# Loading the values of fourteen of sixteen heads through a second DMA queue in a decode attention kernel

## Chip, cores, metric

One core of one Trainium2 chip; the other cores do nothing. The metric is the device time of one execution in microseconds (us). A kernel's time is the median over its runs. The span of a profile, from the first to the last instruction of one profiled execution, is some 1.8 us shorter than the measured time of the same execution.

## The reference, cut to what matters

```python
# x: 2 x 1 x 448; caches: 2 batches x 8 kv heads x 32768 x 256; 16 query heads; bf16
W = 4096                                    # only the last 4096 positions are attended
xn = layernorm(x)
q = (xn @ wq)                               # 448 x 4096
k, v = k_cache[:, :, Sk - W:], v_cache[:, :, Sk - W:]
p = softmax(q @ k.T * Dh ** -0.5)           # each kv head serves two query heads
A = (p @ v) @ wo                            # 4096 x 448
h = xn @ w1 + b1                            # dense part, 448 x 1792
B = (h * tanh(softplus(h))) @ w2
out = x + A + B
```

There are 8 kv heads x 2 batches = 16 "heads" in the kernel, each with one key tile and one value tile of 4096 x 256 bf16, 2.1 MB each. With wq, w1, w2 and wo (0.46 MB for every second head) 77.9 MB have to be read.

## The kernel before

SP (the synchronisation engine, `nc.sync`, which here does nothing but issue transfers) issues all large loads in one order. Keys have 4 buffers and are loaded two heads ahead; values have 5. The timelines show each engine at its own instructions in the order of the program.

```python
k_pool = tc.tile_pool(name="kk", bufs=4)
v_pool = tc.tile_pool(name="vv", bufs=5)     # wq, w1, w2 use these buffers first
...
def load_v(i, cuts=(0, T)):
    ...
    for lo, hi in zip(cuts, cuts[1:]):
        nc.sync.dma_start(out=t[:, lo:hi, :], in_=vin[:, lo:hi, :])
...
for i in range(NK + KA):                     # NK = 16 heads, KA = 2
    if i + 2 < NK:
        load_k(i + 2)                        # nc.sync
    if i < NK:
        load_v(i, ...)                       # the last head's values in three pieces
        if b == Bsz - 1:
            load_wo(kvh, ...)                # nc.sync, every second head
        for half in range(NH):               # two halves of a head
            s = i * NH + half
            turn(s + 1)                      # VectorE: transpose of the NEXT half's keys (L364)
            scores(s)                        # TensorE: 8 matmuls (L376), ACT: exp (L386)
            turn_p(s - 1)                    # VectorE: transpose of p (L397)
            ...
    ...
    if i >= KA:                              # values of head i-2: TensorE, L431
        ...                                  # (last four heads: 64 small matmuls, L479)
    ...                                      # ACT copies o (L439); later wo (L214)
```

The values of head i are used two iterations after its scores.

The softmax here doesn't subtract the row's maximum and nothing guards it: scores larger than these inputs give would overflow.

## Time and profile before

| | before |
|---|---|
| time, median | 190.46 us (190.43 to 190.48) |
| span | 188.7 us |
| bytes | 77.86 MB, 413 GB/s over the span |
| busy: TensorE, VectorE, ACT | 76%, 60%, 17% |
| keys of heads 13, 14, 15 land | 147.80, 158.67, 168.39 us |
| last value piece lands | 184.27 us |

Two rows of the page show how long a transfer stands in line. The columns are: tiles, issuing queue and operation, count, KB each, median us from issue to landing.

```profile
k<-in_A_k_cache_dram SPq DMA_DIRECT2D x16, 2048.0 KB, 31.5
v<-in_A_v_cache_dram SPq DMA_DIRECT2D x15, 2048.0 KB, 34.8
```

A 2.1 MB tile takes 4.9 us at 430 GB/s; over 30 us to landing means that five to six tiles stand before it. The DMA engines are the bound, and one queue keeps them full. The other views (forty slices, the chain of waits, the timelines of VectorE and TensorE) are in the prediction below.

Names in what follows: k14 and v14 are the key and value tile of head 14, counted from 0. "k14 lands" is the start of the first transpose of that tile, where the profile says that VectorE waited for it.

### The profile page before, as it was taken

Reading aid. Unit: us, or ns where it says so; the run is one execution under the profiler, and the core shown is the slowest. Engines: PE = TensorE matmul, PEld = TensorE weight load, DVE = VectorE, ACT = ScalarE, POOL = GpSimd, SP = SyncE. Lnnn points to the kernel's source line nnn. Section 1 sums busy time; section 2 is a strip of 40 time slices with the busy share of each in tenths; the row PEclk is TensorE's granted clock in tenths of the full one; section 3 lists DMA queues with packets and bytes.
Section 4 is the critical chain, followed back from the end, with each engine's and each line's share of the span. In section 5 each row is a group of like instructions: output and inputs, shape, how many; then the busy total and the mean of one; then the engine's idle time right before and its main releaser. Section 6 shows DMA issues by size and latency. Waiting matters only on the chain.

```text
span 188.7 us, 2944 instructions
## 1 busy us (share of the span) xinstructions
PE 144.1 (76%) x1158; PEld 71.7 (38%) x1158; DVE 113.5 (60%) x195; ACT 32.5 (17%) x82; POOL 27.1 (14%) x139
## 2 busy tenths in 40 slices
PE   0152991788995799869985999769986999597782
PEld 0042390234442345334432434324533443254671
DVE  7805505997919392857649381939376673939401
ACT  2300110112212022111222112202311121211101
POOL 8004430033030022003030203003110300000000
PEclk9999995799999699988999699969998799969955
DMA  6999999999999999999999999999999999999991
GB/s 216 423 432 422 430 430 434 438 431 420 417 441 431 420 416 438 441 427 405 442 434 429 434 420 431 434 431 420 431 431 438 412 432 434 431 441 417 408 394 49
DMA packets 7816, 77.86 MB, mean 413 GB/s; under 512 B 757, under 2 KB 2809, under 8 KB 3322
## 3 DMA queue, kind: packets, MB, share of 16 engines
q1 hardware_dynamic: 7796, 77.66, 97.3%
q8 instruction: 9, 0.15, 0.3%
q14 instruction: 5, 0.04, 0.1%
q10 hardware_dynamic: 6, 0.01, 0.0%
HBM read 77.67 MB, written 0.00 MB: 412 GB/s over the span
## 4 chain that ended last, share of the span: by engine, by line
DMA 82%; DVE 11%; issue 2%; PE 2%; SPq 1%; ACT 0%; ACTq 0%
DMA k<-in_A_k_cache_dram 68%; DMA v<-in_A_v_cache_dram 14%; DVE kt L364 8%; DVE pT L397 2%; PE sc L376 1%; SPq L114 0%; PE psA L214 0%; SPq L338 0%; PE q L479 0%; SPq L280 0%; DVE sums L407 0%; SPq L275 0%; DVE sums L404 0%; DVE den_sb L320 0%; ACT p L386 0%
## 5 line engine op out<-in xcount | busy, mean ns | idle before, releaser
L364 DVE STREAM_TRANSPOSE kt<-k 128x2048 f32<-128x2048 f32 x32 | 73.4, 2296 | 50.6 <-DMA k<-in_A_k_cache_dram 49.6
L376 PE MATMUL sc<-kt,qdiag 128*128 128x512 bf16 x256 | 72.7, 433 | 17.6 <-DVE kt L364 15.8
L376 PEld LDWEIGHTS <-qdiag 128*128 128x128 bf16 x256 | 24.7, 105 | 57.2 <-issue 30.0
L431 PE MATMUL o<-v,pT 128*4 128x512 bf16 x192 | 43.4, 379 | 0.0
L264 POOL COPY qdiag<-qrep 32x8 bf16<-32x8 bf16 x128 | 23.1, 213 | 122.4 <-PE sc L376 107.6
L386 ACT ACTIVATE p<-sc 128x512 bf16<-128x512 f32 x32 | 19.1, 597 | 95.6 <-PE sc L376 93.1
L431 PEld LDWEIGHTS <-pT 128*4 128x4 bf16 x192 | 15.8, 87 | 21.8
L397 DVE STREAM_TRANSPOSE pT<-p 128x512 bf16<-128x512 bf16 x32 | 21.5, 672 | 1.1 <-ACT p L386 1.1
L439 ACT COPY o_sb<-o 4x512 f32<-4x512 f32 x12 | 6.9, 574 | 36.8 <-PE o L431 36.8
L214 PE MATMUL psA<-wo,oT 128*2 128x112 bf16 x128 | 3.8, 245 | 11.0 <-DVE oT L447 11.0
L479 PE MATMUL q<-pT,v 128*128 128x2 bf16 x256 | 7.6, 165 | 1.7 <-DMA v<-in_A_v_cache_dram 1.6
L460 PEld LDWEIGHTS q<-ident_f,o_sb 4*128 4x128 f32 x48 | 6.6, 206 | 5.1 <-issue 5.1
L479 PEld LDWEIGHTS <-v 128*128 128x128 bf16 x256 | 7.3, 101 | 2.0 <-DMA v<-in_A_v_cache_dram 2.0
L414 PEld LDWEIGHTS den<-sums,ones_f 128*128 128x128 f32 x32 | 6.8, 220 | 3.3 <-issue 1.7
L460 PE MATMUL q<-ident_f,o_sb 4*128 4x4 f32 x48 | 7.6, 261 | 0.0
L235 PE MATMUL qT_ps<-xs,v 128*128 128x4 bf16 x112 | 3.3, 166 | 4.8 <-DVE ones L201 2.8
L214 PEld LDWEIGHTS <-oT 128*2 128x2 bf16 x128 | 1.8, 87 | 11.9 <-DVE oT L447 11.7
L386 ACT ACTIVATION_READ_ACCUMULATOR p<-sc 128x1 f32 x32 | 6.2, 194 | 0.0
L177 PE MATMUL xnT_ps<-ident,xn_bf 2*128 2x2 bf16 x7 | 0.5, 167 | 6.3 <-DVE xn_bf L139 6.3
L414 PE MATMUL den<-sums,ones_f 128*128 128x2 f32 x32 | 5.1, 229 | 0.0
L235 PEld LDWEIGHTS <-v 128*128 128x128 bf16 x112 | 3.1, 104 | 5.0 <-issue 3.0
L462 DVE COPY osum<-q 128x4 f32<-128x4 f32 x12 | 1.9, 158 | 3.9 <-PE q L460 3.9
(52 smaller groups left out, 46.5 us busy)
## 6 DMA issues: line engine op xcount, KB each, us to landing
k<-in_A_k_cache_dram SPq DMA_DIRECT2D x16, 2048.0 KB, 31.5
v<-in_A_v_cache_dram SPq DMA_DIRECT2D x15, 2048.0 KB, 34.8
v<-in_B_w_dram SPq DMA_DIRECT2D x2, 1568.0 KB, 21.0
wo<-in_A_wo_dram SPq DMA_DIRECT2D x7, 448.0 KB, 31.5
v<-in_A_wq_dram SPq DMA_DIRECT2D x1, 2048.0 KB
v<-in_A_wq_dram SPq DMA_DIRECT2D x1, 1536.0 KB, 10.8
v<-in_A_v_cache_dram SPq DMA_DIRECT2D x1, 1024.0 KB, 29.1
v<-in_A_v_cache_dram SPq DMA_DIRECT2D x2, 512.0 KB, 27.4
```

Of the source, the lines that this page charges most:

```text
L214: nc.tensor.matmul(part(n), lhsT=lhsT, rhs=w[:, n * DO : (n + 1) * DO], start=start, stop=stop, tile_position=(0, n * Q), skip_group_check ...
L235: nc.tensor.matmul(qT_ps[:, hh, e, :], lhsT=wq_v[s][:, hh, e, :], rhs=xs[:, s, :, :].rearrange("p x b -> p (x b)"), start=(s == 0), stop=( ...
L264: nc.gpsimd.tensor_copy(out=tv[rows, :, e, j * Q : (j + 1) * Q : HS], in_=qrep[rows, :, h0 : h0 + rep, e, x, b],)
L364: nc.vector.transpose(out=kt[:].bitcast(FP32), in_=k[:, half * TH * Dh : (half + 1) * TH * Dh].bitcast(FP32),)
L376: nc.tensor.matmul(psc[:], lhsT=qdiag[i % NW][:, n * NE + e, :], rhs=ktv[:, n, e, :, :], start=(n == 0 and e == 0), stop=(n == NB - 1 and ...
L386: nc.scalar.activation(out=p_sb[:], in_=psc[:].rearrange("p t c -> p (t c)"), func=ACT.Exp, scale=scale, accum_out=state["rs", i][:, s % N ...
L397: nc.vector.transpose(out=pT[:], in_=p_t.pop(s)[:])
L414: nc.tensor.matmul(den[:], lhsT=ones_f[:], rhs=state.pop(("sums", i))[:], start=True, stop=True)
L431: nc.tensor.matmul(po[:], lhsT=pT_t[i * NH + half][:, uh * NP * Q : (uh + 1) * NP * Q : HS], rhs=v[:, u * NP : (u + 1) * NP, :].rearrange( ...
L439: nc.scalar.copy(out=o_sb[:], in_=po[:])
L460: nc.tensor.transpose(pqv[:, u, c, :], ov[:, u, c, :], ident_f[0:NR, 0:NR])
L479: nc.tensor.matmul(po[:, c, :], lhsT=vv[:, t, c, :], rhs=pTv[:, th, 0:Q:HS], start=(t == 0 and c == 0), stop=(t == T - 1), skip_group_chec ...
```

## The change

Its intent is to let values travel beside the keys and wo, on a queue of their own. Values of heads 0 to 13 are issued by the Activation engine (ACT), those of heads 14 and 15 stay on SP.

```diff
-    def load_v(i, cuts=(0, T)):
+    def load_v(i, queue, cuts=(0, T)):
...
-            nc.sync.dma_start(out=t[:, lo:hi, :], in_=vin[:, lo:hi, :])
+            queue.dma_start(out=t[:, lo:hi, :], in_=vin[:, lo:hi, :])
...
-            load_v(i, (0, T) if i < NK - 1 else (0, T // 2, 3 * T // 4, T))
+            if i < NK - 2:
+                load_v(i, nc.scalar)
+            elif i < NK - 1:
+                load_v(i, nc.sync)
+            else:
+                load_v(i, nc.sync, (0, T // 2, 3 * T // 4, T))
```

## The prediction

> **What bounds the kernel now.** I read the page first: row 2 (forty slices) and row 3 (the queues), since a decode attention kernel of this kind moves many bytes for little arithmetic.
>
> ```profile
> DMA  6999999999999999999999999999999999999991
> GB/s 216 423 432 422 430 430 434 438 431 420 417 441 431 420 416 438 441 427 405 442 434 429 434 420 431 434 431 420 431 431 438 412 432 434 431 441 417 408 394 49
> ...
> q1 hardware_dynamic: 7796, 77.66, 97.3%
> ```
>
> Slice 1 is half empty, slice 40 almost wholly, and all between carry 394 to 442 GB/s. The queue of SP (q1) has the 16 DMA engines in use for 97.3% of the span. The kernel is bound by its 77.86 MB. Next the chain of waits, for the end:
>
> ```profile
> 127.28 31.36 DMA k<-in_A_k_cache_dram
> 158.64 0.02 issue
> 158.66 25.61 DMA v<-in_A_v_cache_dram
> 184.27 0.05 issue
> 184.31 0.60 PE q L479 x16
> ```
>
> The columns are start, length, what. The last value piece lands at 184.27 and the span ends at 188.7: 4.4 us of tail follow the last byte. Third, the timeline of VectorE, whose transpose of a key tile (L364, two per head) starts as soon as the tile lands:
>
> ```profile
> 147.80 2.31 DVE L364 STREAM_TRANSPOSE kt<-k 128x2048 f32<-128x2048 f32 x1 [3.13 <-DMA k<-in_A_k_cache_dram]
> ...
> 158.67 2.31 DVE L364 STREAM_TRANSPOSE kt<-k 128x2048 f32<-128x2048 f32 x1 [3.43 <-DMA k<-in_A_k_cache_dram]
> ...
> 168.39 2.31 DVE L364 STREAM_TRANSPOSE kt<-k 128x2048 f32<-128x2048 f32 x1 [3.14 <-DMA k<-in_A_k_cache_dram]
> ```
>
> These are heads 13, 14 and 15 (of 0 to 15): their keys land at 147.80, 158.67 and 168.39, and VectorE idles 3.1 to 3.4 us before each. So keys pace the compute, with some 3 us to spare per head. Last, the timeline of TensorE over the end:
>
> ```profile
> 161.12 1.90 PE L376 MATMUL sc<-kt,qdiag 128*128 128x512 bf16 x8 [0.97 <-DVE kt L364]
> ...
> 173.89 1.91 PE L376 MATMUL sc<-kt,qdiag 128*128 128x512 bf16 x8 [1.14 <-DVE kt L364]
> ...
> 179.44 1.87 PE L479 MATMUL q<-pT,v 128*128 128x2 bf16 x64 [0.71 <-DMA v<-in_A_v_cache_dram]
> ...
> 183.09 0.59 PE L479 MATMUL q<-pT,v 128*128 128x2 bf16 x16 [0.21 <-DMA v<-in_A_v_cache_dram]
> 184.31 0.59 PE L479 MATMUL q<-pT,v 128*128 128x2 bf16 x16 [0.63 <-DMA v<-in_A_v_cache_dram]
> ```
>
> At the end TensorE waits for values, not keys, but only 0.71 + 0.21 + 0.63 = 1.55 us in all. The work after the last keys is thus nearly as long as the transfers that cover it. The argument hangs on this small slack.
>
> **What the Trainium skill says.** "DMA: Bandwidth & Descriptors", section "Issuing engines are not separate DMA queues": transfers started by different engines run on the same 16 DMA engines and interleave; a second issuer saves only sequencer time. SP's issues here cost 0.33 to 0.5 us each while the engines have work queued (31.5 us from issue to landing), so that saving is already hidden. Same page, "Where 436 GB/s comes from": a ceiling of 435 GB/s; slices at 430 to 442 agree, and leave nothing to win in rate. Same page, "Queues, rings and completion order": each DMA engine takes its queues in turn, packet by packet. The trace agrees as far as it goes: x, issued on the ACT queue at 0.73 us, is read by VectorE in an instruction that is over at 4.62 us, while the first wq tile, issued on SP at 0.74, holds TensorE until 9.8. A transfer on the second queue does overtake the backlog on the first.
>
> **The change part by part.** Bytes, DMA instructions, arithmetic and buffers stay the same; I checked the order of instructions on each engine as built. Fourteen value loads move from SP to ACT.
>
> Cost of issue: 14 x about 0.35 us = 5 us on ACT, which is 17% busy (32.5 us) and waits 93 us for scores. Off the path: zero.
>
> Waits on ACT: ACT executes in order, and a value load now stands behind the exponentials of head i-1 and the copy of o of head i-3. Its buffer (5 of them) is free by then. Completion semaphores are reused, so some loads also wait for an older transfer, in a few cases the keys of the same head; the exponentials behind need those keys anyway. I count no stall of ACT. But v(i) is now issued only when compute reaches head i, one to two heads later than SP issued it. It is needed two iterations on, some 20 us later, so it is in time.
>
> Order of arrival is what changes. One period of two heads is 147.80 - 127.24 = 20.56 us (key landings of heads 11 and 13) for 4 x 2.097 + 0.459 = 8.85 MB: 430 GB/s, so a key or value tile is 4.88 us and a wo tile 1.07. Before, one FIFO: k14, v12, k15, v13, wo, v14, v15, wo; keys run two heads ahead of values. After, SP holds the key tiles (4 buffers, up to three waiting) and takes turns with ACT's value tile. A value tile gets half the bandwidth as soon as it is issued, and values catch up with keys at the keys' cost. The engines stay full (SP has up to 6 MB, 15 us, queued), so the last byte still lands near 184.3; total bytes decide that.
>
> The start: v0 no longer waits behind k2 but shares with wq, k0, w1, w2 and k1; so k1 lands 4.9 us later. The DMA engines stay busy, so this alone costs nothing at the end.
>
> The end: v13 is through before k15, or nearly. After k15 there remain wo, v14, v15, wo; v13 has gone to the other side of it. Counting back from the same end, k15 lands one tile later: 168.39 + 4.88 = 173.3. For k14 both v12 and most of v13 have moved: with about a third of v13 (1.6 us) still to come, 158.67 + 9.76 - 1.6 = 166.8.
>
> The compute behind them, from the trace of before with waits for transfers taken out:
> - From k15: second score block ends at 175.80, 7.4 us after the landing; to the last L479 without waits 184.91 - 1.55 - 175.80 = 7.6; then 188.7 - 184.9 = 3.8. End: 173.3 + 7.4 + 7.6 + 3.8 = 192.1.
> - From k14, if TensorE then runs without a break: from its first score block to the last L479, 184.91 - 161.12 = 23.8, less waits of 1.14 + 1.55 = 21.1; plus 2.45 for the transpose, plus 3.8. End: 166.8 + 27.35 = 194.2. One score block of that stretch took 3.32 instead of 1.9 us under a lower granted clock; without that, 192.7.
>
> So the span would become 192.1 to 194.2, 3.4 to 5.5 us longer; on the measured 190.46 that is 193.9 to 196.0.
>
> **The rivals.**
> 1. Nothing happens: the last byte comes at 184.3 and the tail keeps its 4.4 us. For it: 97% DMA and the skill's remark. It needs k15 to stay within about 1.6 us of where it was, so that v13 still comes after it: true if the turns are not even, or compute lags so much that v13 is issued late. Time 190 to 191.5.
> 2. A small gain in rate. Slices with wo or other small rows are lower (405 to 420) than the best (441); the wo tiles have rows of 1,792 B, and a second queue could fill behind them. At 436 GB/s, 77.86 MB take 178.6 instead of the 181.8 us between 2.5 and 184.3, but the later keys take back most. Alone: 187.5 to 189.
> 3. Two streams disturb each other in HBM, or ACT blocks on a semaphore and starves the exponentials. Against: nothing shows it before. One per cent of rate costs 1.8 us on top: 195 to 198.
> 4. The main line, the key tiles pushed back and TensorE the bound over the last 20 us: 193.9 to 196.
>
> **Range and chances.** The main line gets about 0.6 of the weight, the first two together 0.3 (that the last two heads are left on SP suggests somebody looked at this end), the third 0.1. The middle is pulled below the main line's: 193.4, range 189.6 to 196.2. The 2% borders are 186.65 and 194.27. Faster by over 2% would need more than the skill's ceiling: 0.02. The upper border cuts the main line, about half of it above: slower 0.38, same 0.60.
>
> **What would show it.** GB/s: still 415 to 442 from slice 2 on, now over two queues, with about 29 MB (14 tiles) on ACT's. Value loads: issue to landing falls from 34.8 us to 10 or so, keys longer or alike. The first transpose of head 15 starts near 173 (168.39 before), that of head 14 near 166 to 167. The last L479 blocks no longer wait for values, and the chain of waits ends in TensorE and VectorE work after a key landing. ACT's waits stay waits for scores. It is wrong if k15 lands before 170 (the turns are not even, or values come late), if the last value lands before 182 (rate gained) or after 186 (rate lost, or starvation), or if ACT shows long waits for transfers.

## The result

The changed kernel takes 194.0 us in the median of 6 runs (193.34 to 196.42; the longest is slow and left out of the ratio), the kernel before 190.47 us (190.39 to 190.74). The ratio is 1.0176, 95% interval 1.0155 to 1.0198. A ratio here is the mean time of one kernel's fast runs over that of the other kernel's fast runs of the same rounds, so it is not quite the ratio of the medians. The loss is clear of noise, and under 2%.

Profile after, forty slices and queues. q1 is SP's queue, q10 ACT's; the columns are packets, MB, share of the 16 engines' span.

```profile
DMA  6999999999999999999999999999999999999940
GB/s 222 425 429 442 414 428 436 434 434 410 444 424 427 424 433 421 434 427 422 434 431 434 420 431 437 420 434 422 432 431 434 420 429 432 437 418 426 406 173 4
...
q1 hardware_dynamic: 5780, 48.30, 59.8%
q10 hardware_dynamic: 2022, 29.37, 35.8%
```

From slice 2 on the rate is what it was. The slices are now 4.8 us wide instead of 4.72, and the transfers end in slice 39 of 40 instead of in slice 40: the bytes are done as early as before, and the run goes on without them. Stretches of two microseconds make that plain. The columns are window, length, then busy time and instruction count of PE (TensorE's matmuls), PEld (its weight loads), DVE (VectorE), ACT and POOL (GpSimd), then the clock granted to TensorE as a share of full speed, DMA share, GB/s. Before:

```profile
182.00:184.00 2.00, 1.47 (x48) 1.30 (x46) 0.00 (x0) 0.00 (x0) 0.00 (x0) 0.50 0.95 378
184.00:186.00 2.00, 1.27 (x32) 0.78 (x32) 0.30 (x2) 0.07 (x1) 0.00 (x0) 0.50 0.30 109
```

After:

```profile
182.00:184.00 2.00, 1.52 (x65) 1.33 (x61) 1.29 (x5) 0.18 (x2) 0.00 (x0) 1.00 0.93 366
184.00:186.00 2.00, 2.00 (x75) 2.00 (x67) 0.17 (x1) 0.00 (x0) 0.00 (x0) 0.84 0.24 92
```

In both the last bytes come between 184 and 185 us. But TensorE, which before had its last 32 matmuls in the second window, now has 75 there and 97 more behind them. The granted clock differs too, but the loss does not come from it: in both profiles one score block of head 14, the second, ran at the half clock (3.32 us before, 3.54 after), and the blocks of values last about as long (1.79 to 1.87 us before, 1.79 to 1.85 after).

VectorE's timeline after, the first transposes of heads 13, 14 and 15 (columns: start, length, engine, line, operation, tiles, count, idle before and what ended it):

```profile
154.48 2.31 DVE L364 STREAM_TRANSPOSE kt<-k 128x2048 f32<-128x2048 f32 x1 [3.13 <-DMA k<-in_A_k_cache_dram]
...
164.82 2.31 DVE L364 STREAM_TRANSPOSE kt<-k 128x2048 f32<-128x2048 f32 x1 [3.02 <-DMA k<-in_A_k_cache_dram]
...
173.34 2.31 DVE L364 STREAM_TRANSPOSE kt<-k 128x2048 f32<-128x2048 f32 x1 [1.93 <-DMA k<-in_A_k_cache_dram]
```

They start 6.7, 6.2 and 5.0 us later than before. TensorE's timeline after, from the first score block of head 14:

```profile
167.28 1.90 PE L376 MATMUL sc<-kt,qdiag 128*128 128x512 bf16 x8 [0.56 <-DVE kt L364]
...
179.54 1.92 PE L376 MATMUL sc<-kt,qdiag 128*128 128x512 bf16 x8 [0.71 <-DVE kt L364]
...
184.24 1.81 PE L479 MATMUL q<-pT,v 128*128 128x2 bf16 x64
...
186.35 1.85 PE L479 MATMUL q<-pT,v 128*128 128x2 bf16 x64
```

The value blocks (L479) carry no wait for values any more. They run one after the other and end at 188.20, where before they ended at 184.90. And the chain of waits, which ended in a value transfer before, now leaves the transfers at k14 (between the third line and the fourth, left out here, it runs over VectorE, ACT and TensorE):

```profile
133.42 31.37 DMA k<-in_A_k_cache_dram
164.79 0.03 issue
164.82 2.31 DVE kt L364
...
184.38 1.68 PE q L479 x64
186.06 0.43 PE den L414 x2
186.48 1.72 PE q L479 x64
```

Issue to landing, after:

```profile
k<-in_A_k_cache_dram SPq DMA_DIRECT2D x16, 2048.0 KB, 31.8
v<-in_A_v_cache_dram ACTq DMA_DIRECT2D x14, 2048.0 KB, 13.8
```

A value tile now lands 13.8 us after its issue instead of 34.8: it goes past the keys that stand in SP's queue. When ACT reaches such an issue will matter below; v13's is here:

```profile
158.91 0.34 ACTq L348 DMA_DIRECT2D v<-in_A_v_cache_dram  x1
```

### The profile page after: what moved, and what is told of

Read it like the earlier page. It is cut to its first block, busy times and chain, and to the rows that moved or that the text cites. A ratio compares the mean times of both kernels' runs of the same rounds, so it can differ in the third digit from the quotient of the medians.

```text
span 191.8 us, 2945 instructions
## 1 busy us (share of the span) xinstructions
PE 146.1 (76%) x1158; PEld 71.8 (37%) x1158; DVE 113.5 (59%) x195; ACT 32.5 (17%) x82; POOL 27.1 (14%) x139
## 3 DMA queue, kind: packets, MB, share of 16 engines
q10 hardware_dynamic: 2022, 29.37, 35.8%
## 4 chain that ended last, share of the span: by engine, by line
DMA 68%; PE 18%; DVE 10%; SPq 1%; issue 1%; ACT 0%; ACTq 0%; DVEq 0%
DMA k<-in_A_k_cache_dram 54%; DMA v<-in_B_w_dram 14%; PE sc L376 9%; DVE kt L364 7%; PE o L431 4%; PE q L479 3%; DVE pT L397 1%; PE psA L214 1%; PE q L460 1%; PE den L414 1%; DVE oT L447 1%; SPq L114 0%; ACT p L386 0%; SPq L275 0%; SPq L338 0%
## 5 line engine op out<-in xcount | busy, mean ns | idle before, releaser
L376 PE MATMUL sc<-kt,qdiag 128*128 128x512 bf16 x256 | 75.5, 446 | 17.7 <-DVE kt L364 17.0
L376 PEld LDWEIGHTS <-qdiag 128*128 128x128 bf16 x256 | 25.2, 107 | 58.8 <-issue 35.0
L386 ACT ACTIVATE p<-sc 128x512 bf16<-128x512 f32 x32 | 19.1, 597 | 102.3 <-PE sc L376 100.3
L479 PEld LDWEIGHTS <-v 128*128 128x128 bf16 x256 | 7.4, 100 | 0.0
L479 PE MATMUL q<-pT,v 128*128 128x2 bf16 x256 | 7.2, 164 | 0.0
## 6 DMA issues: line engine op xcount, KB each, us to landing
v<-in_A_v_cache_dram ACTq DMA_DIRECT2D x14, 2048.0 KB, 13.8
```

The costliest lines, as they stand in the source:

```text
L376: nc.tensor.matmul(psc[:], lhsT=qdiag[i % NW][:, n * NE + e, :], rhs=ktv[:, n, e, :, :], start=(n == 0 and e == 0), stop=(n == NB - 1 and ...
L386: nc.scalar.activation(out=p_sb[:], in_=psc[:].rearrange("p t c -> p (t c)"), func=ACT.Exp, scale=scale, accum_out=state["rs", i][:, s % N ...
L479: nc.tensor.matmul(po[:, c, :], lhsT=vv[:, t, c, :], rhs=pTv[:, th, 0:Q:HS], start=(t == 0 and c == 0), stop=(t == T - 1), skip_group_chec ...
```

## The experiments

Theory A: a value tile on ACT's queue takes turns with SP's queue from about the moment of its issue, so it passes key tiles that were issued before it. The last keys land later by what passed them. The work behind them, which had been just covered by the last transfers, then sets the end. The rivals: B, each issue on ACT costs ACT time, so the loss is spread over the loads; C, two queues disturb each other throughout; D, the late start (k1 lands at 35.01 us instead of 30.34, because v0 shares with it) costs the time.

### One load alone

```diff
-            if i < NK - 2:
+            if i == 13:
                 load_v(i, nc.scalar)
```

> One of the fourteen moved loads alone: v13 on the ACT queue, every other value load on SP as before. Theory A (v13 overtakes k15, so the last keys land one tile later and the compute behind them sets the end): k15 lands near 173.3 us as in the full change (168.4 before), and the time is 193.3 to 194.2, nearly the whole loss from one load. Rival B (issuing on ACT costs ACT time, a fourteenth of the loss): 190.7. Rival C (two queues disturb each other over the whole run): 190.7. Rival D (v0 delays k1 at the start): 190.5.

Measured: 193.44 us against 190.48, ratio 1.0159 (1.0142 to 1.0176). From the profile, the first transposes of heads 14 and 15:

```profile
162.98 2.31 DVE L364 STREAM_TRANSPOSE kt<-k 128x2048 f32<-128x2048 f32 x1 [8.53 <-DMA k<-in_A_k_cache_dram]
...
173.32 2.31 DVE L364 STREAM_TRANSPOSE kt<-k 128x2048 f32<-128x2048 f32 x1 [3.15 <-DMA k<-in_A_k_cache_dram]
```

ACT issued v13 at 150.85 us. k14, on its way at that time, lands 4.3 us later than before, and k15 4.93 us later: one tile. One load of fourteen brings 0.0159 of the 0.0176. B and C would give a fourteenth, and D nothing, as the start is that of the kernel before. All three fall as the main cause.

### Two loads

```diff
-            if i < NK - 2:
+            if i in (12, 13):
                 load_v(i, nc.scalar)
```

> v12 and v13 on the ACT queue, all others on SP. Theory A: as the full change, k14 near 165 and k15 near 173.3 us, time 193.5 to 194.5. B and C: 2/14 of the loss, 191.0. D: 190.5.

Measured: 198.6 us, ratio 1.040 (1.0352 to 1.0449). This is far outside what I expected: two loads cost more than fourteen. The profiled run (196.64 us, span 194.9) tells why the landing is later:

```profile
152.73 2.31 DVE L364 STREAM_TRANSPOSE kt<-k 128x2048 f32<-128x2048 f32 x1 [8.01 <-DMA k<-in_A_k_cache_dram]
...
168.45 2.31 DVE L364 STREAM_TRANSPOSE kt<-k 128x2048 f32<-128x2048 f32 x1 [8.54 <-DMA k<-in_A_k_cache_dram]
```

k13 is 4.93 us later than before, one tile, and k14 is 9.78 us later, two tiles: both v12 and v13 passed it entirely. Here ACT issued v13 at 150.78 us, because compute was still on the schedule of the kernel before; in the full change, where the keys had been late all along, ACT reached that instruction only at 158.91, and k14 had less left to lose. The mechanism is A's, but what counts is the moment of issue against the state of the other queue, not the number of loads. The three timed runs took 2 us more than the profiled one; no trace shows where those went.

### Taking the last loads back

```diff
-            if i < NK - 2:
+            if i < NK - 3:      # label last3_sp: v13 on SP too
+            if i < NK - 4:      # label last4_sp: v12 and v13 on SP too
                 load_v(i, nc.scalar)
```

> The full change, but v13 goes back to SP: thirteen of fourteen loads stay on ACT. Theory A: k15 lands near 168.4 us again, as v13 is behind it again; k14 is still passed by v12 and lands near 160.4 to 163.5, from which the compute chain of 27.0 us (landing of k14 to end in the changed kernel: 164.82 to 191.8) ends at 187.4 to 190.5 where the last values allow 188.7. Time 190.5 to 192.3, middle 191.2. B and C: thirteen fourteenths of the loss stay, 193.7. D: 194.

> v12 and v13 go back to SP: twelve loads stay on ACT. Theory A: from k14 on SP holds the same sequence as before, so k14 near 158.7 and k15 near 168.4 us, time 190.3 to 190.9. B and C: 193.4. D: 194.

Measured: 192.39 us, ratio 1.0110 (1.0070 to 1.0151), with v13 on SP; 192.1 us, ratio 1.0064 (1.0032 to 1.0095), with v12 and v13 on SP (one run of its four slow and left out of the ratio). The loss shrinks as A says and B, C and D do not. But both missed their ranges: the first lies just above (192.39 against 192.3), the second well above (192.1 against 190.9). In the first profile k14 lands at 163.78, and the span is 190.8: 27.0 us after it, as in the full change (164.82 to 191.8). The second profile shows what I had left out. These are the first transposes of heads 12, 13, 14 and 15:

```profile
146.57 2.31 DVE L364 STREAM_TRANSPOSE kt<-k 128x2048 f32<-128x2048 f32 x1 [7.31 <-DMA k<-in_A_k_cache_dram]
...
153.67 2.30 DVE L364 STREAM_TRANSPOSE kt<-k 128x2048 f32<-128x2048 f32 x1
...
162.61 2.30 DVE L364 STREAM_TRANSPOSE kt<-k 128x2048 f32<-128x2048 f32 x1
...
170.54 2.31 DVE L364 STREAM_TRANSPOSE kt<-k 128x2048 f32<-128x2048 f32 x1
```

After k12 VectorE waits for no key: k14 and k15 were there in time. But k12 itself landed 8.5 us late (138.08 before), since the value loads of the heads ahead of it were still on ACT. From k12 on compute runs as fast as it can, 170.54 - 146.57 = 24.0 us for three heads, 8.0 us each against 10.1 for the same three in the kernel before. Three heads make up 6.3 of the 8.5 us, and k15 starts 2.15 us late.

### The same queue, another moment

All fourteen loads stay on ACT; each is issued one head later in ACT's program.

```diff
-            if i < NK - 2:
-                load_v(i, nc.scalar)
-            elif i < NK - 1:
+            if 0 < i < NK - 1:
+                load_v(i - 1, nc.scalar)
+            if i == NK - 2:
                 load_v(i, nc.sync)
+            elif i == NK - 1:
                 ...                              # three pieces, as before
```

> The same fourteen value loads on the ACT queue as in the full change, but each issued one head later in ACT's program (v(i) where v(i+1) stood). Issues on ACT, queues and bytes are those of the full change; only the moment differs. Theory A (refined after the first runs: a value tile on ACT passes every key tile still queued at the moment of its issue; the end comes some 27 us after the start of head 14's first transpose, or 18.5 us after head 15's, whichever is later, but not before the last values allow 188.7): v13 is then issued after k14 has mostly landed, k14 near 162, k15 near 169.5 us, time 190.4 to 191.6. Rivals that blame the ACT issue or two queues in flight: 193.5 to 194.5, as in the full change.

Measured: 190.92 us in the median (190.51 to 192.82), ratio 1.0037 (0.9985 to 1.0088); the profiled run took 191.25. The first transposes of heads 14 and 15:

```profile
160.43 2.31 DVE L364 STREAM_TRANSPOSE kt<-k 128x2048 f32<-128x2048 f32 x1 [4.07 <-DMA k<-in_A_k_cache_dram]
...
170.14 2.31 DVE L364 STREAM_TRANSPOSE kt<-k 128x2048 f32<-128x2048 f32 x1 [3.12 <-DMA k<-in_A_k_cache_dram]
```

v13 is issued when k14 has landed,

```profile
161.40 0.33 ACTq L348 DMA_DIRECT2D v<-in_A_v_cache_dram  x1
```

and k14 and k15 are within 1.8 us of the kernel before. The same 29.37 MB go over ACT's queue as in the full change. So neither the second queue nor the issue on ACT costs the time; the order of arrival does. No difference to the kernel before is shown within the interval, and no gain either.

### The start alone

```diff
-            if i < NK - 2:
+            if i < 8:
                 load_v(i, nc.scalar)
```

> v0 to v7 on ACT, v8 to v15 on SP: the start of the full change with the end of the kernel before. Theory A: k1 lands near 35 us instead of 30.3 and keys of the middle heads come late, but compute is some 2 us faster per head than the transfers, so by head 14 the lateness is gone: k14 near 158.7, k15 near 168.4, time 190.4 to 191.0. Theory D (the late start costs the time): 193.5 to 194.5. Theory B (a share for each load on ACT): 8/14 of the loss, 192.5.

Measured: 190.70 us, ratio 1.0005 (0.9990 to 1.0019), as A expected. Eight loads pass keys and delay them, and compute makes it up, because the ninth value tile and all later ones stand behind their keys again. Starts of the first transposes of heads 8 to 13:

| head | 8 | 9 | 10 | 11 | 12 | 13 |
|---|---|---|---|---|---|---|
| before | 96.99 | 106.67 | 117.56 | 127.24 | 138.08 | 147.80 |
| first eight on ACT | 103.61 | 111.50 | 120.73 | 128.65 | 138.30 | 147.98 |
| later by | 6.6 | 4.8 | 3.2 | 1.4 | 0.2 | 0.2 |

It makes up 1.2 to 1.8 us per head. This settles D, and it says how long the reach of a late key is: some four to five heads.

### Less work behind the last keys

First, half of the score matmuls of heads 14 and 15 are left out, in the changed kernel and in the one before. The results are wrong here and in the next pair (though the outputs of all four runs stayed inside the tolerance of the comparison).

```diff
-        for n in range(NB):
+        nb = NB if i < NK - 2 else NB // 2
+        for n in range(nb):
```

> The full change with half of the score matmuls of heads 14 and 15 left out (the result is wrong on purpose; all transfers stay). If TensorE's work behind the last keys sets the end, some 3.8 us less of it must shorten the run: k15 still near 173.3, but the second score block of head 15 ends 1.8 us earlier, span near 190, time 190.6 to 192.2. If transfers set the end, 194 as before this cut.

> The same cut in the kernel before (result wrong on purpose). There the last values set the end, so the cut only lengthens TensorE's waits for them: time 190.3 to 190.7, nothing gained. If TensorE's work had set the end there too: 187 to 189.

Measured: 192.77 us, ratio 1.0102 (1.0062 to 1.0141), for the changed kernel with the cut; 190.71 us, ratio 1.0007 (0.9992 to 1.0022), for the kernel before with it. The second is as expected, to 0.01 us. The first gained about 1.2 us on the 194.0 of the full change and missed its range. The last three score blocks of the profile, each with four matmuls now:

```profile
171.08 1.04 PE L377 MATMUL sc<-kt,qdiag 128*128 128x512 bf16 x4
...
175.42 1.87 PE L377 MATMUL sc<-kt,qdiag 128*128 128x512 bf16 x4 [1.53 <-DVE kt L364]
178.46 1.89 PE L377 MATMUL sc<-kt,qdiag 128*128 128x512 bf16 x4 [1.18 <-DVE kt L364]
```

The last two take as long as eight matmuls did. The granted clock of TensorE was 0.54 and 0.50 in the windows 174 to 178 and 178 to 182 us, against 0.86 and 1.00 in the full change. The Trainium skill, "TensorE: Matmul & The Clock Gate", Part 1, says that the clock is at half unless recent activity releases it; stretches at 0.50 and at 1.00 agree. That the missing work brought the half clock is not shown: in the last run of this section (half_values_before) the 16 score matmuls of head 15 ran at it too, although nothing ahead of them had been left out (clock 0.51 from 173 to 177 us, 1.00 in the kernel before):

```profile
170.98 6.54 PE L376 MATMUL sc<-kt,qdiag 128*128 128x512 bf16 x16 [0.67 <-DVE kt L364]
```

In the kernel before with this cut, the clock was 0.50 from 169 us on, and the last two score blocks took 1.86 and 1.89 us. So the cut took away little of the time it was meant to in either kernel, and the pair is weak evidence.

Second, every other matmul of the values of heads 13, 14 and 15 is left out. These stand behind the last scores.

```diff
-        for t in range(T):
+        for t in range(1, T, 2) if i >= NK - 3 else range(T):
```

> The full change with every second of the 64 matmuls of the values of heads 13, 14 and 15 left out (result wrong on purpose; all transfers stay). These three groups, 1.8 us each, all run after the last scores. If work behind the last keys sets the end, 3 x 0.9 = 2.7 us go: span near 189.1, time 190.5 to 191.8 against 193.3 to 194.4 for the full change. If transfers or ACT set the end: 193.5 to 194.4.

> The same cut in the kernel before (result wrong on purpose). The last value piece sets the end there, so only the matmuls behind that piece count, 8 fewer of 16, 0.3 us: time 190.0 to 190.5. If TensorE's work set the end there: near 188.

Measured: 192.1 us, ratio 1.0113 (1.0052 to 1.0174), for the changed kernel with the cut; 190.57 us, ratio 1.0003 (0.9988 to 1.0018), for the kernel before with it. The cut takes 1.9 us of median off the changed kernel and nothing off the kernel before, so the work behind the keys sets the end in the one and not in the other. It was less than the 2.7 us expected, because only two of the three groups stood on the path. The first of them and what follows it, in the full change:

```profile
181.43 1.79 PE L479 MATMUL q<-pT,v 128*128 128x2 bf16 x64
183.70 0.37 PE L214 MATMUL psA<-wo,oT 128*2 128x112 bf16 x16 [0.47 <-DVE oT L447]
```

and with the cut:

```profile
181.44 0.97 PE L479 MATMUL q<-pT,v 128*128 128x2 bf16 x32
183.70 0.37 PE L214 MATMUL psA<-wo,oT 128*2 128x112 bf16 x16 [1.29 <-DVE oT L447]
```

The 0.82 us that TensorE saved it spent waiting for VectorE: up to here the chain of waits runs over ACT (the exponentials) and VectorE, and both profiles reach 183.70. The other two groups, 0.84 and 0.86 us shorter, make the 1.7 us between the spans (191.8 and 190.1). In this profile k14 landed 1.2 us later than in the full change (166.00), and it cost nothing: the block at the half clock was the first of head 14 here (3.42 us) and the second there, and both profiles are through the second at 175.3. So the 27.0 us from k14 to the end are no constant. The kernel before with this cut lies just above its range (190.0 to 190.5). There even the 0.3 us behind the last value piece were not gained: the chain of waits of that run ends in the last wo tile,

```profile
168.51 16.99 DMA wo<-in_A_wo_dram
185.50 0.04 issue
185.54 0.46 PE psA L214 x8
```

so two transfers, the last value piece and the last wo piece, stand before the tail of the kernel before, one close behind the other.

### One load more

```diff
-            if i < NK - 2:
+            if i < NK - 1:
                 load_v(i, nc.scalar)
```

> One load more than the full change: v14 on ACT too, issued near 167 us while k15 is still on its way. Theory A: v14 takes half the bandwidth from k15's remaining 3.9 us, k15 lands near 177 instead of 173.3, span 195 to 196, time 196.5 to 198. A theory in which the cost is spread over the loads: one fourteenth more, 194.3.

Measured: 193.33 us in the median (192.88 to 194.93), ratio 1.0162 (1.0118 to 1.0205): no more than the full change, where I expected 196.5 to 198. k15 lands at 175.10 in the profile (the longest of the four runs, span 193.1), 1.8 us later than in the full change and not 4. I had let v14 share from its issue at 166.13 on. But v13, issued at 158.21, was before it in ACT's own queue, with a part still to come, so v14 could share only with the last few microseconds of k15. That is worked out, no view shows it directly. An estimate from the landings, with 4.88 us for a tile and equal turns, fits: k14 at 165.33 is 6.66 us late, of which v12 is 4.88, so 3.1 us of v13 are still to come. They share with k15 until 171.5, k15 then has 1.8 us left, and sharing these with v14 ends at 175.1. Why the timed runs were not even that much longer stays open.

### A second queue at the start

The kernel before, with the second wq tile on ACT's queue:

```diff
-        nc.sync.dma_start(out=w, in_=wq_in[:, lo:hi, :])
+        (nc.sync if lo == 0 else nc.scalar).dma_start(out=w, in_=wq_in[:, lo:hi, :])
```

> The kernel before with the second wq tile alone on the ACT queue, issued near 1.6 us, to see whether a second queue fills the slow start (262 GB/s from 2 to 4 us). It passes no tile that anything waits for, since the projection needs both wq tiles; k0 shares with it. If the start is limited by one queue: up to 0.8 us gained, 189.7 to 190.3. If not: 190.3 to 190.7.

Measured: 190.86 us, ratio 1.0018 (1.0001 to 1.0035), a little above both ranges that I had given. The stretch from 2 to 4 us carries 238 GB/s, not more than the 262 of before, and the first transpose of k0 moves from 16.84 to 19.22 us. A second queue does not fill the slow start. None of the twelve runs beats the kernel before. Its last bytes come before 185 us and its span ends at 188.7, so little seems left to win by order; that is argued, not tried.

### The moment of issue against the landing

Four profiled runs have the same sequence on SP up to k15 and differ by chance or by an edit after it in when ACT reached v13:

| run | v13 issued | k14 lands |
|---|---|---|
| half_values_after | 157.47 | 166.00 |
| last1_sp | 158.21 | 165.33 |
| full change | 158.91 | 164.82 |
| half_scores_after | 160.79 | 163.87 |

3.3 us later issue makes 2.1 us earlier landing. Equal turns would give a microsecond for a microsecond: what is left of k14 takes twice as long from the moment that v13 shares, so a share that begins 1 us later spares k14 1 us. The last row has reached the floor, since k14 landed at 163.78 in last3_sp, where v13 was not on ACT at all. The other three rows give 1.18 us for 1.44, or 0.82: near equal turns, but four traces do not settle it. It is also a reason for the spread of the changed kernel's times (193.34 to 194.38 in fast runs, where the kernel before has 190.39 to 190.74): part of the order is now decided by when compute gets there. This last point is argued from the four traces, not shown for the timed runs.

## Why the prediction was right

- "The engines stay full, so the last byte still lands near 184.3": right in substance; 366 and 92 GB/s from 182 to 186 us against 378 and 109. But 184.27 was the landing of the last value piece. The last wo piece is behind it: the kernel before still moves 240 and 198 GB/s in the two half microseconds from 184 to 185. So less than the 4.4 us of tail follow the last byte; the sums for the end do not use that figure.
- Rate: right; 406 to 444 GB/s in slices 2 to 38 (415 to 442 were forecast), and 29.37 MB on ACT's queue. Single slices lie above the cited ceiling of 435 GB/s, before and after, so it is the mean of some 430 that agrees with it.
- That a second queue overtakes: right (the runs show it), but the lines given for it did not show it. x was issued at 0.73 us, before the first wq tile at 0.74, so there was no backlog to pass; and what TensorE waited for until 9.78 was VectorE (`ones`, L201), not that tile.
- k1 one tile later: 4.67 us (30.34 to 35.01), and without effect on the end (the run with the first eight loads).
- k15 at 173.3: 173.34.
- k14 at 166.8: 164.82. The step that was off is the third of v13 left to come: it was three quarters (158.67 + 9.76 - 164.82 = 3.6 of 4.88 us), as ACT issued v13 only at 158.91.
- The tail: 27.35 us from the landing of k14, measured 27.0. The chain of waits goes by k14, the longer of the two routes that the prediction worked out. It runs over VectorE and ACT as well as TensorE, and as half_values_after shows, the agreement to 0.35 us owes something to which score block fell into the half clock.
- The span: 192.1 to 194.2 on the main line, measured 191.8. The two errors of k14 and of the tail both lie on the low side. The point, pulled down to 193.4 for the rivals, came nearer to the measured 194.0 on the metric than the main line's middle; that is luck, as the rivals it was pulled down for did not happen.
- ACT's waits stayed waits for scores (93.1 before, 100.3 us after), and values came in time: no L479 block waited.
- Off: a value tile lands 13.8 us after its issue, not 10 or so. Half the bandwidth alone makes 9.8 us. The rest need not be the tile before it in ACT's queue: in only_13 v13 had none before it, and equal turns put its first turn some 3.5 us after its issue (158.67 - 4.31 - 150.85, an estimate). What this delay is stays open.
- The loads were treated as if each shifted the keys alike. The run with two loads and the one with v12 and v13 taken back show that what a load costs depends on the moment of its issue, and that lateness is carried for four to five heads. The prediction did not need this; my later expectations did.

## What to carry to other kernels

With the DMA engines full, the second queue moved no more bytes here; it reordered them, and what was issued on the emptier queue passed keys that waited on the other. So before splitting a stream, ask which transfers have the longest work behind them, here the last keys, and let nothing pass those. If a second queue is used all the same, what decides is the moment of issue near the end: the same fourteen loads issued one head later cost nothing that could be shown.

## What the Trainium skill lacked or had wrong

- "DMA: Bandwidth & Descriptors", sections "Issuing engines are not separate DMA queues" and "Rules for kernel authors": they say that spreading over engines does not help and only saves issue time. They lack that it changes the order of arrival, which cost 1.8% here (ratio 1.0176), and 4.0% with two loads alone.
- Same page, "Queues, rings and completion order": that queues take turns is borne out, but the consequence in time is not told. A single 2.1 MB tile on the emptier queue put the last key tile back by 4.93 us, one whole tile, and a tile's issue to landing fell from 34.8 to 13.8 us.
- Same page, "Where 436 GB/s comes from": it says that for transfers from HBM the HBM side, about 358 GB/s, binds. On this one core, with the others idle, every profile here holds about 430 GB/s for 180 us. The 425 GB/s that the same section names for a large transfer agrees with this; the sentence does not.
- "TensorE: Matmul & The Clock Gate", Part 1: agrees, and lacks a warning for experiments that leave out matmuls. At a granted clock of 0.50 four matmuls took 1.87 us where four had taken 1.04 and eight 1.90: read the clock of the stretch before calling work removed, as it differed between profiles even where nothing had been left out (0.51 against 1.00 from 173 to 177 us).
